# Decay factors at the inputs of a filter's layers, and tables of the way back made on GpSimd: a change to a long-convolution kernel with a second block behind it

## Chip, cores, metric

One core of one Trainium2 chip. The metric is the device time of one execution in microseconds (us), the lower the better. A time is given as the median of several executions, with the lowest and highest. Time spent in a stage is read from the profiled execution, one per run. The profiles write PE for TensorE (the matmuls), PEld for its weight loads, DVE for VectorE, ACT for ScalarE, POOL for GpSimd and SP for the queue of transfers; the granted clock is the share of TensorE's full clock that the trace records. A run counts as fast when it lies within 1.5% of the fastest of its kernel.

## The reference

```python
# x, v: (4, 12480, 128)   pos_emb: (12480, 64)   w1: (64, 64)   w2: (64, 128)
h_mlp  = np.maximum(pos_emb @ w1, 0.0) @ w2
window = np.exp(-0.01 * np.arange(S))[:, None]          # decay along the sequence
h_filt = h_mlp * window
u      = x * v
y      = irfft(rfft(u, n=2*S, axis=1) * rfft(h_filt, n=2*S, axis=0))[:, :S]
a      = (x * y).reshape(49920, 128)
h      = a @ w_in                                       # 128 -> 2048
out    = (h * np.cos(h)) @ w_out                        # 2048 -> 128
```

The decay is positive, so max(p, 0) * d = max(p * d, 0): a factor that belongs to a row may be applied to that row of `pos_emb` before the two layers. That is what the change rests on.

## The kernel before

The convolution is a Fourier transform in two steps of sizes 120 and 96, done with matmuls; its way back has two steps too. Sines and cosines ("tables") are made on the chip: each takes an angle, four small elementwise instructions that bring it into range, and a Sin on ScalarE. Everything that the change touches lies in the first 313 of 3840 us. It is made of five stages, called A to E from here on:

- **A**, the filter's layers: eleven chunks of `pos_emb` are transposed, go through `w1` and ReLU; all tables are made beside it; x * v of the first batch begins.
- **B**, the layers' output (`w2`), beside x * v.
- **C**, the first step of the filter's transform, beside the rest of x * v.
- **D**, the first step of the transform of u = x * v, beside the conversion of the second block's weights.
- **E**, the second steps of both transforms, and their product.

```python
def sines(self, row, column, turn, outs, eighths=None):          # class Tables
    base = ...                                    # VectorE: row * column
    for dst, quarters in outs:
        turned = self.pool.tile([P, P], F32, name="turned", bufs=2)
        # four VectorE instructions: moved = base + quarters; turned = moved/turn + ROUND;
        #                            turned = (turned - ROUND)*turn; turned = moved - turned
        yield
        nc.scalar.activation(dst, t, AF.Sin, scale=TWO_PI / turn)

def filter_windows(pool):                         # eleven tables of decay factors
    ...
    for i in range(NCH):
        nc.scalar.activation(w[:, :, :], first[:, :, :], AF.Exp, bias=start[:, i:i+1], scale=DECAY)

def filter_hidden(pool, bank, aT, i, peT, w1_sb, window):
    nc.tensor.matmul(pa[:, 0:ROWS * H], w1_sb[:, :], peT[:, :], start=True, stop=True)
    nc.scalar.activation(t[:, :, :], ..., AF.Relu)
    nc.gpsimd.tensor_tensor(aT[...], t[:, :, :], window[:, :, :], op=ALU.mult)

# A
for i in range(NCH):                              # NCH = 11
    if i + 1 < NCH:
        peTs[i + 1] = filter_turn(pool, bank, pes.pop(i + 1), ident)   # transposes + ScalarE copy
    filter_hidden(pool, bank, aT, i, peTs.pop(i), w1_sb, windows[i])
    for _ in range(2):
        next(sines, None)                         # two tables a round, sixteen in all
    if i >= 5:
        for _ in range(3):
            next(first_u)                         # x * v
...
# C
for i, _ in enumerate(f1_units(bank, ftile[0:FR, :, :, :], f1_evict_filter)):
    if i % 2 == 0:
        next(first_u, None)
```

An eviction copies the result of matmuls out of its accumulation bank, so that the bank can be used again. `f1_units` yields after each half of a channel pair's eviction; even pairs are evicted by ScalarE, odd ones by VectorE. `first_u` yields after each half product and after the sums of a tile of x * v.

Of the kernel before, what the change touches and what calls it, by code (L numbers as in the profile page):

```python
# [16 lines left out]
P = 128  # L17
# [13 lines left out]
def kernel(  # L31
# [62 lines left out]
    KF = N1 - (N2 - N1)  # L94
# [3 lines left out]
    assert NCH * ROWS <= FR <= R and H <= ODD and KE <= 2 * KF and H <= CB and N2 <= P  # L98
# [83 lines left out]
    class Tables:  # L182
        def __init__(self, pool):
            self.pool = pool
            self.prod, self.moved = (
                pool.tile([P, P], F32, name=name) for name in ("prod", "moved"))
# [8 lines left out]
        def sines(self, row, column, turn, outs, eighths=None):  # L195


            p, n = outs[0][0].shape
            base = self.prod[0:p, 0:n]
            nc.vector.tensor_scalar(out=base, in0=row[0:p, 0:n],  # L200
                                    scalar1=column[0:p, 0:1], scalar2=None, op0=ALU.mult)
            if eighths is not None:
                nc.vector.tensor_scalar(out=base[:, eighths], in0=base[:, eighths],
                                        scalar1=float(turn // 8), scalar2=None, op0=ALU.add)
            for dst, quarters in outs:
                turned = self.pool.tile([P, P], F32, name="turned", bufs=2)
                m, t = self.moved[0:p, 0:n], turned[0:p, 0:n]
                if isinstance(quarters, int):
                    quarters = float(quarters * turn // 4)
                nc.vector.tensor_scalar(out=m, in0=base, scalar1=quarters,  # L210
                                        scalar2=None, op0=ALU.add)

                nc.vector.tensor_scalar(out=t, in0=m, scalar1=1.0 / turn, scalar2=ROUND,
                                        op0=ALU.mult, op1=ALU.add)
                nc.vector.tensor_scalar(out=t, in0=t, scalar1=ROUND, scalar2=float(turn),
                                        op0=ALU.subtract, op1=ALU.mult)
                nc.vector.tensor_tensor(t, m, t, op=ALU.subtract)
                yield
                nc.scalar.activation(dst, t, AF.Sin, scale=TWO_PI / turn)

    def tables(pool):

        t = Tables(pool)
        part = t.whole([P, 1], [[1, 1]], channel_multiplier=1, name="part")
        part4 = t.whole([P, 1], [[1, 1]], base=1, channel_multiplier=4, name="part4")
        step = t.whole([P, P], [[1, P]], name="step")
        step4 = t.whole([P, P], [[4, P]], base=1, name="step4")
        mid = t.whole([P, P], [[1, P]], base=-MID, name="mid")
# [17 lines left out]
        yield from t.sines(step4, odd_p, 2 * TURN, [(tw_w[:, 0, :], 1), (tw_w[:, 1, :], 0)])  # L246
        cs, rows, tw_t = back_tables(pool)
# [56 lines left out]
    def filter_windows(pool):  # L304

        first = pool.tile([P, H, ROWS], F32, name="first")
        nc.gpsimd.iota(first[:, :, :], pattern=[[2, H], [N2, ROWS]], base=0,
                       channel_multiplier=0, allow_small_or_imprecise_dtypes=True)
        start = pool.tile([P, NCH], F32, name="start")
        for m in range(2):  # L310
            nc.gpsimd.iota(start[m * FO:(m + 1) * FO, :], pattern=[[ROWS * N2, NCH]], base=m,
                           channel_multiplier=0, allow_small_or_imprecise_dtypes=True)
        nc.vector.tensor_scalar(out=start[:, :], in0=start[:, :], scalar1=DECAY,
                                scalar2=None, op0=ALU.mult)
        windows = []
        for i in range(NCH):
            w = pool.tile([P, H, ROWS], F32, name=f"window{i}")
            nc.scalar.activation(w[:, :, :], first[:, :, :], AF.Exp,
                                 bias=start[:, i:i + 1], scale=DECAY)
            windows.append(w)  # L320
        return windows
# [9 lines left out]
    def filter_hidden(pool, bank, aT, i, peT, w1_sb, window):  # L331

        pa = bank()
        nc.tensor.matmul(pa[:, 0:ROWS * H], w1_sb[:, :], peT[:, :], start=True, stop=True)
        t = pool.tile([P, H, ROWS], F32, name="relu", bufs=2)
        nc.scalar.activation(t[:, :, :], pa[:, 0:ROWS * H].rearrange("p (n a) -> p a n", a=H),
                             AF.Relu)
        nc.gpsimd.tensor_tensor(aT[:, 0:H, i * ROWS:(i + 1) * ROWS], t[:, :, :],
                                window[:, :, :], op=ALU.mult)
# [67 lines left out]
    def f1_evict(ps, b, places=None):  # L407
        copy, negated = f1_takers(b)
        pj = ps[:, 0:4 * N1].rearrange("p (i r k) -> p r k i", i=2, r=2)
        for dst, k in places or ((parts, slice(0, N1)),):  # L410
            copy(out=dst[0:ODD, :, :, b, :], in_=pj[0:ODD, :, k])
        yield
        for dst, k in places or ((parts, slice(0, N1)),):
            copy(out=dst[ODD:KE, 0, :, b, :], in_=pj[ODD:KE, 1, k])
            negated(dst[ODD:KE, 1, :, b, :], pj[ODD:KE, 0, k])
        yield

    def f1_evict_filter(ps, b):
        return f1_evict(ps, b, ((fnear, slice(0, KF)), (ffar, slice(KF, N1))))

    def f2_mm(ps, w, k1, i, filt=False):

        k = k1 + i
        src = parts[:, :, k] if not filt else fnear[:, :, k] if k < KF else ffar[:, :, k - KF]
        nc.tensor.matmul(ps[0:N2, i * 2 * D:(i + 1) * 2 * D], w[:, i, :], src[0:KE],  # L425
                         start=True, stop=True)
# [304 lines left out]
    with tc.manual_schedule():  # L731
        with tc.tile_pool(name="psum", bufs=8, space=PSUM) as psum, \
# [8 lines left out]
            ffar = above.rearrange("p b (r k) i -> p r k b i", r=2)  # L741
# [6 lines left out]
            with tc.tile_pool(name="layers", bufs=1, side="right") as pool:  # L748
# [8 lines left out]
                for i in range(1, NCH):  # L757
                    pes[i] = filter_load(pool, i)
                first_u = u_units(0, 3, slots[0:R, :, :, :],
                                  lambda j, half: nc.gpsimd if half == 0 or 6 <= j < 18  # L760
                                  else nc.vector)
# [3 lines left out]
                windows = filter_windows(pool)  # L765
                sines = tables(pool)
                nc.gpsimd.memset(aT[:, 0:H, NCH * ROWS:FR], 0.0)
                peTs = {0: filter_turn(pool, bank, pes.pop(0), ident)}
                for i in range(NCH):
                    if i + 1 < NCH:  # L770
                        peTs[i + 1] = filter_turn(pool, bank, pes.pop(i + 1), ident)
                    filter_hidden(pool, bank, aT, i, peTs.pop(i), w1_sb, windows[i])
                    for _ in range(2):
                        next(sines, None)
                    if i >= 5:
                        for _ in range(3):
# [5 lines left out]
            ftile = fpool.tile([P, CB, 2 * KF, 2], F32, name="ftile")  # L782
            fnear = ftile[:, :, :, :].rearrange("p b (r k) i -> p r k b i", r=2)
            clear_gap(ftile[0:FR, :, :, :])
            with tc.tile_pool(name="out", bufs=1, side="right") as pool:
                for j in range(H // 2):
                    filter_out(pool, bank, aT, ftile, j, w2_sb)
                    for _ in range(1 + (j % 4 == 0)):
                        next(first_u)
            for i, _ in enumerate(f1_units(bank, ftile[0:FR, :, :, :], f1_evict_filter)):  # L790
                if i % 2 == 0:
                    next(first_u, None)
            for _ in first_u:
                pass
# [113 lines left out]
```

## Time and profile before

Time before: 3840.26 us (3834.36 to 3843.71, three runs); the profiled run spans 3838.6 us. The stage borders are the first matmul of each stage in the trace (of the output, the filter's first step, u's first step, the second steps, the way back). The views that carry the bounds are shown in the prediction.

| stage | begins, us | length, us | what sets its end |
|---|---|---|---|
| A layers | 0 | 52.19 | eleven exponentials, then rounds of two tables on VectorE, then GpSimd |
| B output | 52.19 | 32.03 | GpSimd |
| C filter, first step | 84.22 | 65.43 | VectorE until 122, then matmuls at half clock (0.50 from 121.70 to 147) |
| D u, first step | 149.65 | 58.02 | matmuls, VectorE and the conversion |
| E second steps | 207.67 | 105.41 | VectorE beside TensorE |
| way back of batch 0 | 313.08 | 82.95 | not touched |
| second block begins | 396.03 | | not touched |

From 15.6 to 43 us VectorE never stands for as long as 0.15 us, so it is its own work that sets the rounds. But seven times, once for each product of GpSimd's with the decay, a small instruction of VectorE's takes 1.0 to 1.9 us where its like take 0.2 to 0.3, and ends just after that product; together some 7 us (an estimate: their lengths in the trace less those of their like). One of the seven, in the timelines of GpSimd and VectorE:

```profile
24.98 1.21 POOL L338 TENSOR_TENSOR slots<-relu,window 128x480 f32<-128x480 f32 x1 [2.23 <-ACT relu L336]
25.17 1.07 DVE L210 TENSOR_SCALAR moved<-prod 120x61 f32<-120x61 f32 x1
```

### The profile page before, as it was taken

The page shows a single profiled execution, that of the slowest core. Times are in us where ns is not written, and L with a number is a line of the kernel's source. Part 1 is how long each engine was busy: PE and PEld are TensorE (multiplying, and loading weights), DVE is VectorE, ACT ScalarE, POOL GpSimd, SP SyncE. Part 2 cuts the span into 40 slices and gives each one's busy share as a digit, 9 for nine tenths or more (in the row PEclk, how much of TensorE's full clock was granted, in tenths as well). Part 3 has the DMA queues.
Part 4 walks back from the last instruction along what each step waited for, and adds up shares of the span by engine and source line. Part 5 has one row for each costly group of instructions (what it writes and reads, how often), then busy time and mean ns, then how long its engine had stood idle before and what let it go on. Part 6 is the DMA issues. An engine that isn't in the chain of part 4 may idle for free.

```text
span 3838.6 us, 47111 instructions
## 1 busy us (share of the span) xinstructions
PE 3728.1 (97%) x13450; PEld 2119.9 (55%) x13450; DVE 2819.6 (73%) x5803; ACT 2494.4 (65%) x4639; POOL 2551.1 (66%) x2274
## 2 busy tenths in 40 slices
PE   6988889999999999999999999999999999999999
PEld 4867444655556555645566556555566544444444
DVE  7888798678876787687766887788765566666666
ACT  4654566766666556766665557666654677777777
POOL 6365677478864665588845665688644577777776
PEclk8899999999999999999999999999999999999999
DMA  4253443022210561022202640122105300000000
GB/s 135 61 147 100 147 138 104 12 60 73 78 40 17 171 183 48 24 77 72 77 12 82 180 140 17 51 77 77 51 17 155 90 17 17 22 17 23 17 17 17
DMA packets 209082, 274.64 MB, mean 72 GB/s; under 512 B 17062, under 2 KB 146486, under 8 KB 208694
## 3 DMA queue, kind: packets, MB, share of 16 engines
q1 hardware_dynamic: 208822, 271.63, 24.2%
q8 instruction: 108, 1.77, 0.2%
q14 instruction: 152, 1.25, 0.1%
HBM read 191.93 MB, written 79.63 MB: 71 GB/s over the span
## 4 chain that ended last, share of the span: by engine, by line
PE 84%; DVE 5%; POOL 4%; ACT 3%; DMA 2%; issue 2%; SPq 0%; DVEq 0%; POOLq 0%; ACTq 0%
PE ph L677 32%; PE acc L702 27%; PE cv L702 5%; PE cv L468 5%; PE cv L443 4%; PE cv L395 3%; PE cv L425 3%; POOL f L686 2%; PE ph L126 2%; PE ps L395 1%; DMA hd<-h 1%; PE ps L443 1%; DVE k L683 1%; ACT cs L691 1%; DVE gt L693 1%
## 5 line engine op out<-in xcount | busy, mean ns | idle before, releaser
L686 POOL TENSOR_TENSOR f<-a,k 128x512 f32<-128x512 f32 x1568 | 1989.7, 1269 | 1065.2 <-DVE k L683 1064.1
L677 PE MATMUL ph<-at,w_in_sb 128*128 128x512 f32 x3136 | 1600.8, 592 | 20.0 <-DVE gt L693 19.6
L680 ACT ACTIVATE a<-ph,quarter 128x512 f32<-128x512 f32 x1568 | 1073.2, 684 | 746.7 <-PE ph L677 737.1
L702 PE MATMUL acc<-gt,w_out_sb 128*128 128x512 f32 x2656 | 1359.7, 593 | 5.6 <-ACT ot L708 5.3
L693 DVE TENSOR_TENSOR gt<-ph,cs 128x512 f32<-128x512 f32 x1568 | 1077.7, 687 | 326.7 <-ACT cs L691 299.3
L691 ACT ACTIVATE cs<-f 128x512 f32<-128x512 f32 x1568 | 980.3, 625 | 370.7 <-POOL f L686 369.0
L683 DVE TENSOR_SCALAR k<-a 128x512 f32<-128x512 f32 x1568 | 782.4, 499 | 595.0 <-ACT a L680 577.6
L702 PEld LDWEIGHTS acc<-gt,w_out_sb 128*128 128x128 f32 x2656 | 500.0, 189 | 650.3 <-issue 613.6
L677 PEld LDWEIGHTS ph<-at,w_in_sb 128*128 128x128 f32 x3136 | 553.2, 190 | 359.2 <-issue 262.3
L438 POOL TENSOR_TENSOR slots<-slots,t 120x256 f32<-120x256 f32 x384 | 310.7, 815 | 62.1 <-DVE t L437 23.8
L468 PEld LDWEIGHTS cv<-slots,tm 96*104 96x104 f32 x1920 | 241.5, 171 | 99.0 <-issue 86.0
L468 PE MATMUL cv<-slots,tm 96*104 96x128 f32 x1920 | 253.5, 275 | 3.8 <-DVE tm L277 3.8
L702 PE MATMUL cv<-gt,w_out_sb 128*128 128x512 f32 (+1 forms) x480 | 238.5, 579 | 1.0 <-DVE gt L693 1.0
L443 PEld LDWEIGHTS cv<-cs,slots 120*96 120x96 f32 x1536 | 176.9, 167 | 69.1 <-issue 68.7
L443 PE MATMUL cv<-cs,slots 120*96 120x120 f32 x1536 | 183.2, 266 | 0.0
L425 PE MATMUL cv<-slots,w 124*120 124x256 f32 x576 | 173.0, 380 | 0.0
L425 PEld LDWEIGHTS cv<-slots,w 124*120 124x120 f32 x576 | 103.4, 184 | 122.4 <-issue 109.7
L395 PEld LDWEIGHTS cv<-c,slots 104*124 104x124 f32 x768 | 132.7, 192 | 64.4 <-issue 58.3
L702 PEld LDWEIGHTS cv<-gt,w_out_sb 128*128 128x128 f32 x480 | 90.9, 190 | 110.2 <-issue 106.9
L395 PE MATMUL cv<-c,slots 104*124 104x192 f32 x768 | 150.9, 326 | 0.1
L383 DVE TENSOR_TENSOR xt<-xt,vt 104x256 f32<-104x256 f32 x198 | 146.7, 743 | 1.2 <-DMA vt<-in_v_dram 0.9
L453 DVE TENSOR_TENSOR slots<-cv,other 96x240 f32<-96x240 f32 x384 | 133.6, 394 | 2.8 <-ACT other L451 2.8
(116 smaller groups left out, 2549.0 us busy)
## 6 DMA issues: line engine op xcount, KB each, us to landing
h<-hd SPq DMA_DIRECT2D x144, 240.0 KB
tm<-td SPq DMA_DIRECT2D x90, 312.0 KB
xt<-in_x_dram SPq DMA_DIRECT2D x120, 208.0 KB
vt<-in_v_dram SPq DMA_DIRECT2D x120, 208.0 KB
xs<-in_x_dram SPq DMA_DIRECT2D x120, 208.0 KB
zd<-zs SPq DMA_DIRECT2D x120, 208.0 KB
zb<-zd SPq DMA_DIRECT2D x97, 256.0 KB
w<-wd SPq DMA_DIRECT2D x144, 116.2 KB
```

The costliest lines, as they stand in the source:

```text
L395: nc.tensor.matmul(ps[0:KE, i * 2 * N1:(i + 1) * 2 * N1], u[:, b, 0:KE, i], c1[0:u.shape[0], :, :].rearrange("p r k -> p (r k)"), start=Tr ...
L425: nc.tensor.matmul(ps[0:N2, i * 2 * D:(i + 1) * 2 * D], w[:, i, :], src[0:KE], start=True, stop=True)
L438: nc.gpsimd.tensor_tensor(y[:, r], y[:, r], t[:, r], op=op)
L443: nc.tensor.matmul(ps[0:N1, (i * 2 + r) * N2:(i * 2 + r + 1) * N2], parts[0:N2, r, :, b, i], cs[:, r, :], start=True, stop=True)
L468: nc.tensor.matmul(ps[0:R, i * D:(i + 1) * D], t[:, i, r, :], slots[0:N1, :, place, :], start=(r == 0), stop=(r == 1))
L677: nc.tensor.matmul(ph[:, 0:m], w_in_sb[:, c * P:(c + 1) * P], ats[n][:, 0:m], start=True, stop=True)
L680: nc.scalar.activation(a[:, 0:m], ph[:, 0:m], AF.Identity, bias=quarter[:, 0:1], scale=INV_TWO_PI)
L683: nc.vector.tensor_scalar(out=k[:, 0:m], in0=a[:, 0:m], scalar1=ROUND, scalar2=ROUND, op0=ALU.add, op1=ALU.subtract)
L686: nc.gpsimd.tensor_tensor(f[:, 0:m], a[:, 0:m], k[:, 0:m], op=ALU.subtract)
L691: nc.scalar.activation(cs[:, 0:m], f[:, 0:m], AF.Sin, scale=TWO_PI)
L693: nc.vector.tensor_tensor(gt[:, 0:m], ph[:, 0:m], cs[:, 0:m], op=ALU.mult)
L702: nc.tensor.matmul(accs[n][:, 0:m], w_out_sb[:, c, :], gt[:, 0:m], start=(c == 0), stop=(c == NFC - 1))
```

## The change

The intent has four parts. The decay goes to the inputs: one exponential instead of eleven, and VectorE multiplies each chunk of `pos_emb` in place before the transposes, so ReLU writes its result directly. Ten of the sixteen tables, those of the way back, leave A and are made on GpSimd in C, after x * v. x * v itself begins a round earlier, with a new split of its products between VectorE and GpSimd, and takes two steps a round. A new layout of the filter's tile saves one VectorE or ScalarE instruction of six per channel pair, and splits the second step's matmul in two for the values of k from 48 on.

```diff
 class Tables:
-    def __init__(self, pool):
+    def __init__(self, pool, engine):                 # every nc.vector below -> self.engine
-def tables(pool):                                     # sixteen tables
-    t = Tables(pool)
+def forward_tables(pool):                             # six
+    t = Tables(pool, nc.vector)
+def inverse_tables(pool):                             # ten
+    t = Tables(pool, nc.gpsimd)
...
-def filter_windows(pool):                             # eleven Exp
+def filter_window(pool):                              # one Exp, 120 x 88
+def filter_scale(pe, window, i):
+    w = window[:, i * ROWS:(i + 1) * ROWS]
+    spread = bass.AP(tensor=w.tensor, offset=w.offset, ap=[*w.ap, [0, FO]])
+    nc.vector.tensor_tensor(rows, rows, spread, op=ALU.mult)
...
 def filter_hidden(...):
-    nc.scalar.activation(t[:, :, :], ..., AF.Relu)
-    nc.gpsimd.tensor_tensor(aT[...], t[:, :, :], window[:, :, :], op=ALU.mult)
+    nc.scalar.activation(aT[...], ..., AF.Relu)
...
 def f1_evict_filter(ps, b):
-    return f1_evict(ps, b, ((fnear, slice(0, KF)), (ffar, slice(KF, N1))))   # six instructions
+    copy(out=near[0:ODD], in_=pj[0:ODD, 0:N1 + KF])
+    copy(out=far[0:ODD], in_=pj[0:ODD, N1 + KF:])
+    yield
+    copy(out=near[ODD:KE, 0:N1], in_=pj[ODD:KE, N1:])
+    negated(near[ODD:KE, N1:], pj[ODD:KE, 0:KF])
+    negated(far[ODD:KE], pj[ODD:KE, KF:N1])
...
 # A
-first_u = u_units(..., lambda j, half: nc.gpsimd if half == 0 or 6 <= j < 18 else nc.vector)
+first_u = u_units(..., lambda j, half: nc.vector if half and j % 3 else nc.gpsimd)
...
+for i in range(NCH + 1):
+    if i < NCH:
+        pe = pes.pop(i)
+        filter_scale(pe, window, i)
+        peTs[i] = filter_turn(pool, bank, pe, ident)
+    if i > 0:
+        filter_hidden(bank, aT, i - 1, peTs.pop(i - 1), w1_sb)
+    next(sines, None)                                 # one table a round
+    if i >= 4:
+        for _ in range(2):
+            next(first_u)
...
 # C
+f1 = f1_units(bank, ftile[0:FR, :, :, :], f1_evict_filter)
+for _ in first_u:
+    for _ in range(2):
+        next(f1)
+with tc.tile_pool(name="tables", bufs=1) as pool:
+    sines = inverse_tables(pool)
+    for i, _ in enumerate(f1):
+        if i % 5 == 0:
+            next(sines, None)
+    for _ in sines:
+        pass
```

## The prediction

> **What bounds the kernel now.** I read the page first, then the span cut at the borders between stages, then in each stage the chain of waits and each engine's timeline.
>
> ```profile
> PE 3728.1 (97%) x13450; PEld 2119.9 (55%) x13450; DVE 2819.6 (73%) x5803; ACT 2494.4 (65%) x4639; POOL 2551.1 (66%) x2274
> ```
>
> TensorE is busy 97% of the span. The diff touches nothing after the first way back begins (about 313 us), so only the opening can change. Its stages, found from where each line's matmuls begin and end (columns: stretch, length, then busy us of PE, PEld, DVE, ACT, POOL; granted clock, DMA share, GB/s):
>
> ```profile
> 0.00:52.20 52.20, 26.49 (x67) 12.98 (x67) 32.88 (x87) 23.32 (x51) 23.63 (x38) 0.74 0.43 110
> 52.20:84.20 32.00, 27.79 (x120) 20.46 (x121) 26.74 (x75) 11.05 (x30) 30.38 (x39) 0.93 0.58 168
> 84.20:121.70 37.50, 35.45 (x176) 32.95 (x176) 32.94 (x121) 25.97 (x132) 20.66 (x28) 0.86 0.46 131
> 121.70:149.65 27.95, 26.59 (x81) 23.12 (x81) 20.78 (x90) 11.49 (x60) 0.58 (x1) 0.53 0.08 28
> 149.65:207.00 57.35, 46.59 (x258) 44.68 (x256) 47.80 (x128) 40.83 (x122) 28.56 (x32) 0.93 0.15 42
> 207.00:313.00 106.00, 96.86 (x384) 67.58 (x384) 92.82 (x288) 52.91 (x138) 67.53 (x96) 0.97 0.58 169
> ```
>
> These are: A, the filter's layers (0 to 52); B, the layers' output beside x * v (52 to 84); C, the filter's first step, with x * v until 122 and alone after that; D, the same step of u; E, both second steps. B is GpSimd's (30.4 of 32.0). In C, VectorE is first the bound, then the matmuls at about half clock. The chain through A:
>
> ```profile
> 3.44 6.55 ACT window L318 x11
> 9.99 0.45 ACT peT L328
> 10.48 1.98 PE ps L334 x2
> 12.49 0.58 ACT relu L336
> 13.14 1.20 POOL slots L338
> 14.34 0.18 POOL part L190 x2
> ...
> 18.61 1.04 DVE turned L213
> ```
>
> Eleven exponentials hold ScalarE for 6.5 us, so the first copy waits until 10. GpSimd, in order, waits for the first ReLU before it makes the counts for the tables, so VectorE's tables start at 15. Eight rounds of two tables then take 3.3 us each, until 43. From 43 to 52 a third limit follows:
>
> ```profile
> 43.89 0.97 POOL L389 TENSOR_TENSOR slots<-xt 104x256 f32<-104x256 f32 x1 [2.80 <-DVE xt L383]
> 44.82 1.20 POOL L338 TENSOR_TENSOR slots<-relu,window 128x480 f32<-128x480 f32 x1
> ...
> 44.19 2.10 DVE L383 TENSOR_TENSOR xt<-xt,vt 104x256 f32<-104x256 f32 x1
> ```
>
> GpSimd runs three instructions back to back per round (3.07 us), and VectorE's product, 0.42 us elsewhere, takes 2.10 beside them.
>
> [...] VectorE's difference at 68.39 kept its 0.42 beside a GpSimd sum that began 0.04 us later and took 0.97 for 0.73[...]. [...] the matmuls of 127.83 to 149.65 run without a gap, and the clock stays at 0.50 until 147.
>
> ```profile
> 127.83 21.99 PE L395 MATMUL ps<-c,ftile 96*124 96x192 f32 x68 [1.29 <-ACT slots L402]
> ```
>
> **A, the layers.** Removed: eleven exponentials (6.55 us of ScalarE), eleven GpSimd products (11 x 1.20 = 13.2 us), and ten of sixteen tables from VectorE (24.7 to 43.1 us, x * v in between). Added: one exponential of 120x88 and eleven VectorE products of 120x512 at 0.69 us = 7.6 us. The first product can start when its input has landed (3.76 us, from the first transpose), the second at 7.05 (the second transpose's wait for DMA). From there, per round, VectorE has 0.7 + 1.2 for one table (a product or none, then four instructions at 0.24) = 1.9 us; TensorE at half clock has 0.8 for four transposes + 1.6 for the layer = 2.4, and about 1.4 at full; ScalarE 0.45 + 0.47 + 0.2 = 1.1. I take 2.2: round 6 starts at 7 + 5 x 2.2 = 18. In rounds 6 to 11 there is no table, but two thirds of an x * v tile: VectorE 0.7 + 0.5, GpSimd 1.3 to 1.4 (products 0.72 x 4/3 + sum 0.97, times 2/3). [...] 2.3 to 2.5 us. Six rounds at 2.3 end at 18 + 14 = 32, and the last ReLU at about **33**, against 52.2: **-19 us**.
>
> **B, the output.** 40 steps of x * v instead of 38, 13.3 tiles instead of 12.7. Before, a tile with both products on GpSimd takes 1.41 + 0.97 = 2.42 us. Now GpSimd has 1.9 on average, but VectorE has, per tile, 2.25 pairs of outputs at 0.69 = 1.55, plus 0.43 x 2/3 + 0.43 = 0.72, plus gaps: about 2.4. The bound changes engine but not size: 13.3 x 2.4 = 32 us. **+1 us** at most.
>
> **C, the filter's first step.** Its evictions have five instructions for six (60x192 in place of 60x144 and 60x48): from start to start 1.45 us become about 1.34 on VectorE for each odd channel pair. VectorE's products in x * v fall by a third. With x * v: 1.5 x 1.34 + 0.8 = 2.8 us a tile against 3.1; 11.7 tiles save 3.5 us. The rest are 30 channel pairs, and beside them GpSimd now makes ten tables. Its tensor_scalar costs (start to start 0.08 more):
>
> ```profile
> L135 POOL TENSOR_SCALAR power<-power 128x256 uint32<-128x256 uint32 x16 | 17.2, 1077 | 74.9 <-DVE power L133 41.3 <-DVE sig L141 33.6
> L280 POOL TENSOR_SCALAR spare<-rows,tw_t 96x208 f32<-96x208 f32 x30 | 27.0, 899 | 0.4
> L147 POOL TENSOR_TENSOR sig<-sig,low 128x256 f32<-128x256 f32 x16 | 11.6, 727 | 1.3
> ```
>
> The first two lie on one line of 0.15 us + 3.6 ns an element, though one has two operations and the other one. With the gap: 0.61 us at 104, 0.66 at 120, 0.45 at 60; a tensor_tensor 0.33 to 0.46. Four tables of 60 columns make 7.8 us, four of 104 make 9.6, two of 120 make 5.8; with four counts, 24 us. ScalarE's sine for each sits in its queue five half steps after the last, so it follows GpSimd at 2.5 pairs per 2.4 us = 0.96 us a pair, 24 us, plus some 3 for the last pairs. Before, the stretch alone took 28 (29 pairs, half clock at 1.46 us a pair once TensorE had lost its lead). So what the first part wins, the tables or the cold clock may take: **-1 us**, with room from -8 to +5.
>
> **D and E.** The raw weights now land in memory that the tables held, so their loads wait until these are stored: some 6 us after C, where the first conversion wants them 5 us into D. **+1 us.** In E the filter's matmuls for k from 48 on are split in two, 128 columns for 256: 48 more matmuls, 96 more instructions. In the way back, 100 matmuls of 120 columns pass in 10 us (320 to 330) with as many weight loads beside them, so two halves at 0.107 cost what one at 0.218 does, and E runs at VectorE's 2.04 us a step anyway (DVE 18 to 19 of every 20 us). **+1 us.**
>
> **Sum.** -19 + 1 - 1 + 1 + 1 = -17: 3840 - 17 = 3823 us.
>
> **Rivals.** (1) The gain of A is lost in C: the clock stays at half through C, or ScalarE waits for slow tables. [...] C would grow by 8 us: 3832. [...] (3) The clock stays full: then C ends with VectorE (32 x 1.34 + 9.4 + 3 = 55 us) and the tables (about 60), 5 us earlier: 3817. (4) Split matmuls bound by weight loads (0.18 each when alone): 24 steps x 0.5 less the slack of 0.3 = +5 us; the way back speaks against it.
>
> **Range and chances.** The runs of before spread by 9 us. With 8 us of doubt in A and 7 in C: 3808 to 3837 should hold it 8 times in 10. Two per cent is 77 us; faster than that would need stages A and B to vanish, slower has no cause in sight. Faster 0.01, same 0.98, slower 0.01.
>
> **What would show it.** Right: one exponential; the first output matmul at 30 to 36 us; the output stage 31 to 33 us long with VectorE busy over 90%; the tables on GpSimd 22 to 26 us long, ScalarE's sines waiting for them; E's steps at 2.04 to 2.1. Wrong: products over 1.5 us in A; the last matmul of the filter's first step more than 70 us after its first; E longer than 110 us; or a change after 313 us beyond some 5 us.

The sum keeps all its terms, -19 + 1 - 1 + 1 + 1 = -17. Two of its figures have to be read with their source. The 0.69 us of VectorE's products is the 690 ns of a 128x512 product in the profile before (L693, mean). The 2.3 us a round in A's second part is the estimate: it lays the 1.2 us of VectorE and the 1.3 to 1.4 of GpSimd mostly end to end, as at 44.19, where VectorE's product took 2.10 us beside GpSimd's work; that they always delay each other so was not shown. Rival (2) had A's products long beside GpSimd's work from the fourth round on, as at 44.19, and A ending at 42: 3833 us. Rival (1) keeps its size but not its argument, a figure for the use of TensorE that no view shows: the trace has matmuls for 8.51 of the 10 us from 106 to 116, at a clock of 1.00, then 0.59 until 121.70 and 0.50 until 147.

## The result, and the profile after

| | median, us | lowest to highest | runs |
|---|---|---|---|
| before | 3841.99 | 3834.36 to 3849.87 | 4 |
| after | 3821.43 | 3814.44 to 3823.07 | 4 |

The ratio is 0.9943, with a 95% interval of 0.9919 to 0.9967: the class is "same" by the 2% rule, though the interval excludes 1, so that a gain is clear of the noise. Here and below a ratio is that over the fast runs of both kernels, and not quite the ratio of the medians quoted. The profiled runs span 3838.6 and 3819.3 us, at a mean granted clock of 0.985 and 0.989.

The page of the kernel after, part 1, in the same columns as before (busy us, share of the span, instructions):

```profile
PE 3713.3 (97%) x13546; PEld 2117.3 (55%) x13546; DVE 2804.5 (73%) x5737; ACT 2488.4 (65%) x4597; POOL 2559.8 (67%) x2307
```

The span of the kernel after, cut at its own stage borders A to E (columns as in the prediction: stretch, length, busy us of PE, PEld, DVE, ACT, POOL; granted clock, DMA share, GB/s):

```profile
0.00:30.70 30.70, 18.13 (x67) 8.96 (x67) 17.18 (x48) 16.25 (x31) 14.26 (x25) 1.00 0.68 168
30.70:63.40 32.70, 26.11 (x120) 19.48 (x121) 30.04 (x83) 11.05 (x30) 27.57 (x32) 0.95 0.59 174
63.40:124.57 61.17, 52.83 (x256) 49.05 (x257) 51.51 (x177) 37.90 (x166) 43.45 (x81) 0.83 0.30 85
124.57:182.41 57.84, 44.50 (x257) 43.16 (x257) 48.13 (x128) 41.31 (x123) 28.59 (x32) 0.94 0.19 56
182.41:288.00 105.59, 97.22 (x480) 74.27 (x480) 91.41 (x286) 52.91 (x138) 66.78 (x94) 0.98 0.58 168
```

Stage A lost nearly 16 us of VectorE and 9 of GpSimd. In B the busiest engine is now VectorE (30.04 of 32.70 us, 92%), where it was GpSimd, at the same length. Put side by side:

| stage | before | after | predicted change | measured change |
|---|---|---|---|---|
| A | 52.19 | 30.70 | -19 | -21.5 |
| B | 32.03 | 32.70 | +1 | +0.7 |
| C | 65.43 | 61.17 | -1 | -4.3 |
| D | 58.02 | 57.84 | +1 | -0.2 |
| E | 105.41 | 106.57 | +1 | +1.2 |
| way back of batch 0 | 82.95 | 83.58 | 0 | +0.6 |
| second block, to its first finished tile | 52.51 | 55.50 | 0 | +3.0 |
| all after that | | | 0 | +1.2 |
| sum | | | -17 | -19.3 |

**A.** The chain of waits through A of the kernel after (start, length, what), against the one of before in the prediction:

```profile
7.21 0.70 DVE pe L323
...
9.01 1.63 PE ps L336 x2
...
11.25 1.28 ACT L219
...
16.65 0.83 PE ps L336 x2
```

The eleven exponentials are gone from the chain. L323 is the new product, L336 the layer, and the 1.28 us on ScalarE is the load of the Sin table, which stands before the first sine. This load makes one round long: VectorE waits 2.95 us for that sine, and the fourth product starts 4.86 us after the third. From 16 us the layer takes 0.83 us instead of 1.63, the pace of a full clock, and the first output matmul is at 30.70. (The clock column shows 1.00 for all of A; the durations say that the matmuls until about 12 us ran at half of it.) From the seventh round on x * v runs beside the products. The timelines of GpSimd and VectorE there (start, duration, engine, line, operation, count, and in brackets the idle time before and what ended it):

```profile
18.82 1.94 POOL L382 TENSOR_TENSOR xt<-xt,vt 104x256 f32<-104x256 f32 x2 [15.52 <-DMA vt<-in_v_dram]
20.84 1.57 POOL L388 TENSOR_TENSOR slots<-xt 104x256 f32<-104x256 f32 x1
22.37 1.51 POOL L382 TENSOR_TENSOR xt<-xt,vt 104x256 f32<-104x256 f32 x1
...
18.96 1.22 DVE L323 TENSOR_TENSOR pe<-pe,window 120x512 f32<-120x512 f32 x1
22.62 0.68 DVE L323 TENSOR_TENSOR pe<-pe,window 120x512 f32<-120x512 f32 x1
```

GpSimd stands until 18.82 because the first tile of v has not landed, however early the program asks for x * v. From then on it runs without a gap until 30.4, and four of its ten operations are slowed: three sums take 1.57 us where the others take 0.97, and a product 1.51 where the others take 0.70 to 0.97. VectorE's product with the decay was slowed once (1.22 for 0.69) and then kept its time; its two products of x * v took 0.95 instead of 0.42. Which of two instructions that overlap was the longer did not go with which began first: here GpSimd's product of 22.37 us took 1.51 and VectorE's, which began 0.25 us later, kept its 0.68; in the kernel before, VectorE's instruction of 25.17 us, which began 0.19 us after GpSimd's, took 1.07 for 0.2. A's end follows the landing of v: in the nine runs whose tables of the way back are off VectorE in A and whose decay is at the inputs, GpSimd's first product starts between 18.8 and 20.3 us, and A ends 10.9 to 12.1 us after it (in the kernel after 18.82 and 30.70, in e6 19.73 and 31.50). No run moved that landing.

**C.** ScalarE's and GpSimd's timelines in the kernel after, where x * v ends and the tables begin:

```profile
92.05 0.23 ACT L421 COPY slots<-ps 64x96 f32<-64x96 f32 x1
103.27 0.26 ACT L219 ACTIVATE cs<-turned 120x61 f32<-120x61 f32 x1 [10.99 <-POOL turned L217]
...
99.04 0.97 POOL L388 TENSOR_TENSOR slots<-xt 104x256 f32<-104x256 f32 x1 [0.74 <-DVE xt L382]
109.50 0.48 POOL L210 TENSOR_SCALAR moved<-prod 96x104 f32<-96x104 f32 x1
110.06 0.28 POOL L213 TENSOR_SCALAR turned<-moved 96x104 f32<-96x104 f32 x1
110.42 0.58 POOL L215 TENSOR_SCALAR turned<-turned 96x104 f32<-96x104 f32 x1
122.53 0.44 POOL L217 TENSOR_TENSOR turned<-moved,turned 96x120 f32<-96x120 f32 x1
```

GpSimd's last sum of x * v starts at 99.04; then it makes counts and tables from 100.09 to 122.97, 22.9 us. ScalarE had run ahead of it: it was done with its share of the pairs up to the first sine at 92.3, and stood there for 10.99 us. TensorE needs an empty bank for every pair. While ScalarE stands, only VectorE empties banks, and each of its evictions lets one pair through (four matmul records):

```profile
98.49 1.64 PE L394 MATMUL ps<-c,ftile 96*124 96x192 f32 x4 [1.65 <-DVE slots L403]
104.21 6.12 PE L394 MATMUL ps<-c,ftile 96*124 96x192 f32 x18 [1.72 <-ACT slots L401]
```

So TensorE's waits from 90 to 102 us are put down to VectorE (six, 4.3 us), and only that at 104.21 to ScalarE. TensorE starves, and the clock falls at about 97.5 (1.00 from 95 to 97 us, 0.50 from 98 to 104). That ScalarE's standing is behind this is shown by e3 below. A window of the same kernel over that stretch (the last three figures are clock, DMA share and GB/s):

```profile
97.00:111.00 14.00, 10.08 (x29) 9.01 (x30) 11.53 (x41) 6.67 (x29) 11.51 (x30) 0.52 0.03 9
```

**The second block's start.** Nothing there was changed, and 3 us were given back. TensorE's timeline of the kernel after, and then of the kernel before, at the same place (L691 after is L677 before, L716 is L702):

```profile
381.24 1.09 PE L126 MATMUL ph<-ident,zb 128*128 128x128 f32 x4 [2.58 <-DMA zb<-zd]
383.83 1.91 PE L691 MATMUL ph<-at,w_in_sb 128*128 128x512 f32 x2
388.31 1.02 PE L716 MATMUL acc<-gt,w_out_sb 128*128 128x512 f32 x2
```

```profile
404.88 0.63 PE L126 MATMUL ph<-ident,zb 128*128 128x128 f32 x4 [3.02 <-DVE xt L383]
407.10 1.02 PE L702 MATMUL acc<-gt,w_out_sb 128*128 128x512 f32 x2
```

Both stand for 2.6 to 3 us before the transposes. After this, the pairs of matmuls take 1.91 us in the kernel after (half clock, 0.50 from 381 to 387 us) and 1.02 in the kernel before. From the second tile to the last the distance between the two kernels stays between 18.8 and 20.2 us; it is 19.3 at the end.

### The profile page after: what moved, and what is told of

It reads as the page before. It is cut to its first block, busy times and chain, and to the rows that moved or that the text cites. A ratio compares the mean times of both kernels' runs of the same rounds, so it can differ in the third digit from the quotient of the medians.

```text
span 3819.3 us, 47226 instructions
## 1 busy us (share of the span) xinstructions
PE 3713.3 (97%) x13546; PEld 2117.3 (55%) x13546; DVE 2804.5 (73%) x5737; ACT 2488.4 (65%) x4597; POOL 2559.8 (67%) x2307
## 4 chain that ended last, share of the span: by engine, by line
PE 85%; DVE 5%; POOL 3%; DMA 3%; ACT 2%; issue 2%; SPq 0%; DVEq 0%; POOLq 0%; ACTq 0%
PE ph L691 32%; PE acc L716 28%; PE cv L716 5%; PE cv L482 5%; PE cv L457 4%; PE cv L394 3%; PE cv L433 3%; PE ph L126 2%; POOL f L700 2%; DMA hd<-h 2%; PE ps L457 1%; ACT cs L705 1%; DVE k L697 1%; PE ps L394 1%; DVE xt L382 1%
## 5 line engine op out<-in xcount | busy, mean ns | idle before, releaser
L691 PE MATMUL ph<-at,w_in_sb 128*128 128x512 f32 x3136 | 1602.7, 592 | 18.6 <-DVE gt L707 18.2
L716 PE MATMUL acc<-gt,w_out_sb 128*128 128x512 f32 x2656 | 1362.4, 594 | 5.5 <-ACT ot L722 5.3
L716 PEld LDWEIGHTS acc<-gt,w_out_sb 128*128 128x128 f32 x2656 | 500.9, 189 | 651.2 <-issue 614.1
L691 PEld LDWEIGHTS ph<-at,w_in_sb 128*128 128x128 f32 x3136 | 553.9, 190 | 358.3 <-issue 262.9
L716 PE MATMUL cv<-gt,w_out_sb 128*128 128x512 f32 (+1 forms) x480 | 238.5, 579 | 1.0 <-DVE gt L707 1.0
L716 PEld LDWEIGHTS cv<-gt,w_out_sb 128*128 128x128 f32 x480 | 90.9, 190 | 110.2 <-issue 106.9
```

The costliest lines, as they stand in the source:

```text
L691: nc.tensor.matmul(ph[:, 0:m], w_in_sb[:, c * P:(c + 1) * P], ats[n][:, 0:m], start=True, stop=True)
L716: nc.tensor.matmul(accs[n][:, 0:m], w_out_sb[:, c, :], gt[:, 0:m], start=(c == 0), stop=(c == NFC - 1))
```

## The experiments

Eleven runs, all correct against the reference: ten kernels, and the changed kernel once more. The theory to be tested: the gain is stage A's, and needs both parts; in C the tables on GpSimd are the new limit; the rest (split matmuls, share of x * v) costs little. The rivals stand in the expectations. Stages are read from one profile a run; what the same program varies by is seen in after_again. "f2" below is the moment of the first matmul of E, so the sum of A to D.

| kernel | A | B | C | D | C+D | f2 at | span |
|---|---|---|---|---|---|---|---|
| before | 52.19 | 32.03 | 65.43 | 58.02 | 123.45 | 207.67 | 3838.6 |
| after | 30.70 | 32.70 | 61.17 | 57.84 | 119.01 | 182.41 | 3819.3 |
| e1_decay_only | 51.77 | 33.23 | 50.04 | 63.07 | 113.11 | 198.11 | 3835.6 |
| e2_tables_only | 40.57 | 31.92 | 66.33 | 58.63 | 124.96 | 197.45 | 3831.7 |
| e3_sines_last | 31.08 | 33.50 | 50.29 | 69.86 | 120.15 | 184.73 | 3815.3 |
| e4_old_share | 30.57 | 34.21 | 64.40 | 58.01 | 122.41 | 187.19 | 3819.6 |
| e5_more_buffers | 38.55 | 33.40 | 50.30 | 62.95 | 113.25 | 185.20 | 3822.4 |
| e6_cs_in_layers | 31.50 | 33.55 | 58.34 | 58.37 | 116.71 | 181.76 | 3815.4 |
| e7_old_places | 31.40 | 32.77 | 64.59 | 58.43 | 123.02 | 187.19 | 3823.7 |
| e8_warm_start | 31.12 | 32.78 | 61.17 | 57.88 | 119.05 | 182.95 | 3815.9 |
| after_again | 30.96 | 32.96 | 61.07 | 58.27 | 119.34 | 183.26 | 3816.2 |
| e9_both | 31.02 | 33.34 | 52.77 | 61.39 | 114.16 | 178.52 | 3815.7 |
| e10_all | 32.14 | 33.33 | 52.76 | 61.85 | 114.61 | 180.08 | 3812.1 |

| kernel | median, us (lowest to highest, runs) | before in the same rounds | ratio (95%) |
|---|---|---|---|
| e1_decay_only | 3834.90 (3833.76 to 3837.80, 4) | 3840.44 | 0.9988 (0.9973 to 1.0003) |
| e2_tables_only | 3833.62 (3833.03 to 3838.16, 4) | 3840.44 | 0.9987 (0.9971 to 1.0004) |
| e3_sines_last | 3819.64 (3817.09 to 3822.84, 4) | 3840.44 | 0.9948 (0.9933 to 0.9963) |
| e4_old_share | 3823.62 (3821.36 to 3824.67, 4) | 3840.44 | 0.9957 (0.9942 to 0.9972) |
| e5_more_buffers | 3824.66 (one run, state unknown) | 3842.10 | |
| e6_cs_in_layers | 3816.98 (3815.47 to 3817.30, 4) | 3842.10 | 0.9929 (0.9913 to 0.9946) |
| e7_old_places | 3825.47 (one run, state unknown) | 3842.10 | |
| e8_warm_start | 3819.78 (3817.75 to 3820.60, 4) | 3842.10 | 0.9937 (0.9922 to 0.9952) |
| after_again | 3820.49 (3818.09 to 3823.01, 6) | 3841.76 | 0.9941 (0.9927 to 0.9954) |
| e9_both | 3815.58 (3811.81 to 3817.49, 4) | 3841.76 | 0.9926 (0.9911 to 0.9940) |
| e10_all | 3813.91 (3812.36 to 3814.49, 5) | 3841.76 | 0.9922 (0.9907 to 0.9937) |

### e1_decay_only: the change, with the ten tables back on VectorE in A

```diff
-    t = Tables(pool, nc.gpsimd)
+    t = Tables(pool, nc.vector)                        # in inverse_tables
-sines = forward_tables(pool)
+sines = itertools.chain(forward_tables(pool), inverse_tables(pool))
-    next(sines, None)
+    for _ in range(2):
+        next(sines, None)
 # and in C, no tables: "for _ in f1: pass"
```

> The changed kernel, but the ten tables of the way back are made on VectorE in the layers' stage again, as before the change (two tables a round). Theory: the decay at the inputs and the move of the tables win separately. The layers' stage then has 8 rounds of 0.65 + 2.5 us instead of 2 us, so its end moves from 30.7 to about 41 to 43 us; the filter's first step loses its tables and with them ScalarE's wait, so it shrinks from 61.2 to about 56. At the start of the second steps the kernel is then some 6 us behind the changed one (182.4 becomes 187 to 190), in all 12 to 16 us faster than before. Rival (the tables' move is nearly the whole gain): the layers' stage ends at 48 or later and the kernel is within 6 us of before.

A took 51.77 us: the theory missed, and the rival it named for A held. The decay at the inputs, here with the new share of x * v and the new layout, gains 0.4 us in A. Timelines of ScalarE and VectorE of this kernel, over one of the rounds:

```profile
33.97 0.56 ACT L331 COPY peT<-ps 128x480 f32<-128x480 f32 x1 [2.44 <-PE ps L127]
...
32.06 0.68 DVE L324 TENSOR_TENSOR pe<-pe,window 120x512 f32<-120x512 f32 x1
36.30 0.21 DVE L214 TENSOR_SCALAR turned<-moved 96x104 f32<-96x104 f32 x1 [2.33 <-ACT rows L220]
```

Read as a ring: VectorE's product at 32.06 releases the transposes, these release ScalarE's copy at 33.97, the layer and the ReLU follow, and only behind them in ScalarE's queue come the round's two sines, at 35.99. VectorE at 36.30 has waited 2.33 us for a sine, because the table it is about to write goes into one of two `turned` buffers, which the sine has to free. Only after that comes the next product. A round takes 4.89 us (27.17 to 32.06 from product to product), longer than the 3.3 us of before, where no product of VectorE's stood ahead of the transposes. So the new product lengthens the very loop that the old tables keep, which the theory's expectation didn't see. (VectorE's small instructions, seven of which took 1.0 to 1.9 us beside GpSimd's products before, take 0.2 to 0.3 us in this round.) In C + D, on the other hand, this kernel has 113.11 us, 10.3 less than before: what C and D take when no tables lie beside them.

### e5_more_buffers: e1 with six `turned` buffers instead of two

```diff
-turned = self.pool.tile([P, P], F32, name="turned", bufs=2)
+turned = self.pool.tile([P, P], F32, name="turned", bufs=6)
```

> The kernel of the run that kept the tables on VectorE in the layers' stage (first output matmul at 51.8 us), with six buffers for the sines' inputs instead of two. There each round took 4.9 us: the second table of a round waits 1.5 to 2.3 us for the sine that frees its buffer, and that sine queues on ScalarE behind a copy and a ReLU that hang on VectorE's own product of the same round. Theory: the ring of VectorE, TensorE, ScalarE through two buffers costs the 10 us, not the tables' work; with six buffers a round is 0.65 + 2.5 = 3.2 us and the output begins at 38 to 43 us. [...]

(The rival had A stay at 49 to 52 us, with VectorE's own work as one limit.) A fell from 51.77 to 38.55 us, within what the buffers' theory expected: the ring is through the buffers. (More buffers in the kernel before were not tried; there VectorE hardly waits in these rounds, so they have no wait to remove.) It also says what moving the tables to GpSimd buys beyond that. Against e5, the kernel after is 7.9 us shorter in A and 0.7 in B, and 5.8 longer in C + D (119.01 against 113.25): it is at f2 only 2.8 us earlier.

### e2_tables_only: before, with only the ten tables moved to GpSimd in C

```diff
-sines = tables(pool)
+sines = forward_tables(pool)                           # Tables as in the change
-    for _ in range(2):
-        next(sines, None)
+    next(sines, None)
 # and C as in the change; the windows and GpSimd's products stay
```

> The kernel before, with only the tables of the way back moved to GpSimd beside the filter's first step (one table a round in the layers' stage). Theory: the exponentials still hold the first copy until 10 us and GpSimd still makes eleven products, so from round 5 on GpSimd sets 3.07 us a round; the layers' stage ends at 43 to 46 us instead of 52.2. The filter's first step has the same wait of ScalarE for GpSimd's tables as the changed kernel and lasts 60 to 65 us. In all 5 to 11 us faster than before. Rival (the tables on VectorE were what held the layers' stage): it ends at 38 or earlier and most of the changed kernel's gain is there.

A took 40.57 us, 11.6 less than before: below the 43 to 46 expected and above the rival's 38. C took 66.33 us, above the 60 to 65 expected, and C + D grew by 1.5 us over before: the old eviction is still there and the tables are added. With e1 this makes the square in A complete, if one leaves aside that e1 has the new share and layout too (taken out of the changed kernel alone, by e4 and e7, they move A by -0.1 and +0.7): decay alone -0.4, tables alone -11.6, both -21.5. The parts alone add up to -12.0, which is 9.5 us short of both together. The whole kernels follow: 0.9988 and 0.9987 for the parts (both intervals contain 1), 0.9943 for the change.

### e3_sines_last: the change, with the ten sines only after the filter's last pair

```diff
-turned = self.pool.tile([P, P], F32, name="turned", bufs=2)
+turned = self.pool.tile([P, P], F32, name="turned", bufs=10 if late else 2)
...
-    yield
-    nc.scalar.activation(dst, t, AF.Sin, scale=TWO_PI / turn)
+    if late: self.owed.append((dst, t, TWO_PI / turn))
+    yield
+    if not late: nc.scalar.activation(dst, t, AF.Sin, scale=TWO_PI / turn)
 # all owed sines after the last unit of f1
```

> The changed kernel, but ScalarE's ten sines of the way back are emitted after the last unit of the filter's first step, with ten buffers between, so no eviction queues behind a sine that waits for GpSimd. Theory: the 11 us in which ScalarE stands before the first sine (92 to 103 us) starve TensorE of banks and bring the half clock at 97 to 111; without them the first step of the filter is bound by VectorE and lasts 55 to 58 us instead of 61.2; the sines then wait for GpSimd's last table once (ScalarE free again at about 123 to 125 us), which u's first step pays with 0 to 2 us. In all 2 to 6 us faster than the changed kernel. Rival: VectorE's backlog or the half clock sets the end of the stage anyway; then it stays at 60 to 62 us and the total within 1 us.

C became 10.9 us shorter, even more than the theory of ScalarE's wait expected, but D 12.0 longer, so the expected 2 to 6 us for the whole were missed: C + D is 120.15 us against 119.01. Lines of ScalarE's timeline and of the table of waits of this kernel (114 to 185 us; who waited, for whom, in total, times, longest):

```profile
124.07 0.30 ACT L267 ACTIVATE tw_t<-turned 96x120 f32<-96x120 f32 x1 [1.89 <-POOL turned L218]
...
PE ps L401 <- ACT slots L408: 8.5, 1, 8.5
```

Now ScalarE waits for GpSimd's last table at the end instead of for the first one at the beginning, TensorE waits 8.5 us for it, and ScalarE begins D's evictions only at 124.39. In C TensorE now waits 1.7 us in all for ScalarE and 0.8 for VectorE (its start aside), and the clock stays at 1.00 from 84 to 116 us: so it was ScalarE's standing that starved TensorE in the kernel after. Yet the time only moved on into D; the wait at the front is therefore not itself the cost. What sets the end is GpSimd's chain, x * v to 100 and then 23 us of tables, wherever the sines stand.

### e6_cs_in_layers: the four smaller tables on GpSimd already in A

```diff
+def cs_tables(pool):                                   # the four tables of 60 columns,
+    t = Tables(pool, nc.gpsimd, lag=2)                 # each sine two rounds after its table
+    ...
 # A, once a round:
     next(sines, None)
+    next(more, None)                                   # more = cs_tables(pool)
 # in C, six tables are left
```

> The changed kernel, with four of the ten tables of the way back (the 60-column ones, 8.6 us of GpSimd) made on GpSimd in the layers' stage, where it has nothing to do from 3.3 to 18.8 us; their sines follow two rounds later. Six remain beside the filter's first step. Theory: from the last x * v tile (about 100 us) GpSimd's tables are the chain that ends the filter's first step and holds ScalarE, whatever the place of the sines; with 15 us of them for 24, that step and u's first step together take 112 to 116 us instead of 119[...]. In all 3 to 7 us faster than the changed kernel. Rival (VectorE's evictions and the conversions of u's first step set the sum): the two steps stay at 118 to 120.

C + D fell to 116.71 us, against 119.01, and just missed the range expected; A cost 0.8 us (31.50 against 30.70; 0 to 2 were expected). The whole kernel takes 3816.98 us. The shorter chain pays, as the reading of e3 says it must, but ScalarE still stands before its first sine of C; the waits of this kernel from 64 to 122 us:

```profile
ACT rows L226 <- POOL turned L218: 12.1, 3, 10.9
```

### e9_both: e6, with the six remaining sines last, and the addition written as x * 1.0 + c

```diff
-self.engine.tensor_scalar(out=m, in0=base, scalar1=quarters, scalar2=None, op0=ALU.add)
+self.engine.tensor_scalar(out=m, in0=base, scalar1=1.0, scalar2=quarters,
+                          op0=ALU.mult, op1=ALU.add)   # where quarters is a number
 # e6's six tables in C: sines after the last unit of f1, as in e3
```

> The changed kernel with both: four tables in the layers' stage on GpSimd, and the six remaining sines only after the last unit of the filter's first step; besides, the addition of a quarter turn is written as times 1 plus a constant, since GpSimd's times-and-plus took 0.28 us on 96x104 where its plus alone took 0.48. Theory: each alone left the other's wait (alone, the later sines moved the wait into u's first step; alone, the fewer tables left ScalarE standing 10.9 us before the first sine). Together GpSimd is done at 115 to 117 us, when VectorE ends the filter's first step; that step and u's take 108 to 112 us instead of 119, and the kernel is 6 to 11 us faster than the changed one. Rival (u's first step is bound by the conversions started late): the two take 115 or more.

C + D is 114.16 us, against 119.34 in the run of the changed kernel beside it (after_again): 5.2 us won, though not the 108 to 112 expected. That range was set below what there was to win, for e1 and e5, without any tables in C, have 113.1 and 113.3; e9 has all but 1 us of it. What each of the three parts of the edit gives in e9 isn't separated. The odd part of it shows in GpSimd's timeline of this kernel, a line to be compared with the one at 109.50 of the kernel after, which took 0.48 us for the same addition on the same shape:

```profile
102.19 0.27 POOL L212 TENSOR_SCALAR moved<-prod 96x104 f32<-96x104 f32 x1
```

The end is less clear than the stage: of the 6 us that e9 was ahead where the second block begins, only 0.5 us are left in the two profiled spans, since that block took 54.68 us to its first tile instead of 52.58 and lost more by 555 us. The timed runs show 3815.58 against 3820.49 us, and their ranges don't overlap.

### e4_old_share: the change, with x * v shared as before

```diff
-lambda j, half: nc.vector if half and j % 3 else nc.gpsimd
+lambda j, half: nc.gpsimd if half == 0 or 6 <= j < 18 else nc.vector
```

> The changed kernel with the old share of x * v between GpSimd and VectorE (second halves on GpSimd for tiles 6 to 17, on VectorE for the others). Theory: the output stage is 32 to 33.5 us either way, bound by GpSimd at 2.42 us a tile instead of by VectorE, and the filter's first step is 1 to 2 us longer because VectorE has every second half there; in all 0 to 3 us slower than the changed kernel. Rival (the spread share is what made room): the output stage grows by over 3 us.

B became 1.5 us and C 3.2 us longer, 4.8 at f2, more than the 0 to 3 expected. With the old split every second half of the tiles from 18 on lies on VectorE, which in C has the evictions too. In the profiled span it doesn't show: that is 3819.6 us, as in the kernel after, because in this run the second block started in 52.30 us and not in 55.50. In the timed runs the median is 16.8 us below before of the same rounds, where the changed kernel's is 20.6 and 21.3 below; the intervals of the ratios overlap.

### e7_old_places: the change, with the old layout of the filter's tile and unsplit matmuls

```diff
-KF = N1 - 2 * (N2 - N1)
+KF = N1 - (N2 - N1)
 # f1_evict, f1_evict_filter and f2_mm as before: six instructions a pair, one matmul for all k
```

> The changed kernel with the filter's old places: six evictions a channel pair, one matmul of 256 columns for every k. Theory: 1.45 us for 1.36 on VectorE per odd pair, so the stretch with x * v grows by some 1.6 us and with it the start of the tables; the filter's first step 62 to 64 us instead of 61.2, the second steps unchanged at 105 to 107.5 us whatever the matmuls, since VectorE sets them. Rival (split matmuls cost): the second steps fall below 105.

C took 64.59 us instead of 61.17, a little above the range expected, so the sixth instruction was worth 3.4 us there. E took 106.34, against 106.57 with the split matmuls: a cost of the split doesn't show, and the 5 us of the prediction's fourth rival are ruled out.

### e8_warm_start: the change, with unread matmuls before the second block's first transposes

```diff
 load(0)
+keep_warm(10)                # 128x512 matmuls of w_in with itself; nobody reads the result
 moe_turn(mpool, 0)
...
+if c == LAG - 1 and n == 0:
+    keep_warm(3)
```

> The changed kernel with thirteen matmuls more whose result nobody reads, ten while TensorE waits for the first rows of the second block and three while it waits for the next ones. Theory: the 3 us that the changed kernel gave back between the second block's first matmul and its first finished tile (55.5 us for 52.5) are half clock at 382 to 387; with TensorE kept busy that stretch is 49 to 52.5 us, and the kernel 2 to 6 us faster. Rival (a transfer or a wait holds the stretch): it stays at 55 to 56 us while the clock is full.

TensorE's timeline of this kernel:

```profile
376.29 3.48 PE L872 MATMUL ph<-w_in_sb 128*128 128x512 f32 x6
...
383.11 1.02 PE L716 MATMUL acc<-gt,w_out_sb 128*128 128x512 f32 x2
```

After the unread matmuls the real ones take 1.02 us, and the clock in the stretch to the first finished tile is 1.00 where the kernel after has 0.93. The stretch took 53.16 us, more than the 49 to 52.5 expected, though the block also began 2.5 us earlier (81.08 us after the way back's start, not 83.58). From f2 to the first finished tile this makes 4.4 us less than in the kernel after. After_again has the same program as the kernel after, no unread matmuls, and 52.58 us for the same stretch at a clock of 0.99. The stretch in the kernel after, in after_again and in e8 (columns as before):

```profile
372.56:428.06 55.50, 48.81 (x179) 27.06 (x178) 46.96 (x80) 32.34 (x65) 39.20 (x37) 0.93 0.47 137
373.42:426.00 52.58, 45.54 (x179) 25.00 (x178) 46.63 (x80) 32.32 (x65) 39.66 (x37) 0.99 0.49 145
371.07:424.23 53.16, 47.90 (x186) 25.79 (x184) 47.14 (x82) 33.17 (x68) 38.23 (x37) 1.00 0.48 143
```

So the 3 us that the change seemed to give back differ between two runs of the same program, and are not the change's. The lower clock goes with them here, but that it alone sets the stretch isn't shown: e3 has 52.34 us at 0.96. Nor is it shown that unread matmuls make the kernel faster: the medians, 3819.78 us and 3820.49 in after_again, are from different rounds, and the ratios are 0.9937 and 0.9941.

### after_again: the changed kernel once more, beside e9 and e10

> The changed kernel once more, for rounds shared with the two that follow. Theory: the stages' borders repeat to a few tenths of a us except where the clock differs; 0.994 to 0.995 of the kernel before.

A to D repeat within 0.5 us each, and so does E; the second block's start is 2.9 us shorter. Beside the kernel before of the same rounds the median is 21.3 us lower (ratio 0.9941).

### e10_all: e9, with the unread matmuls and a third `turned` buffer for the tables of A

```diff
-t = Tables(pool, nc.vector)
+t = Tables(pool, nc.vector, lag=1)      # in forward_tables: one sine later, three buffers
 # and keep_warm as in e8
```

> The previous one with the matmuls [...] at the start of the second block, and with a third buffer and one round of delay for the forward tables' sines, so that VectorE doesn't stand 2.9 us in the third round. Theory: the second block's start wins 3 to 4 us as before, the layers' stage 0 to 2.5 us; 9 to 16 us faster than the changed kernel, 0.990 to 0.992 of the kernel before. Rival: the layers' stage is then held by x * v's first transfer (18.8 us) and wins nothing.

A didn't gain: 32.14 us against 31.02 in e9. Its rounds end with x * v on GpSimd, which here starts when v has landed at 20.26 us, and A ends 11.9 us later, as in the kernel after; so an earlier table has nothing to move, as the rival had it. The test isn't a clean one, though: the third buffer didn't remove VectorE's wait for the first sine, it came one table later and took 3.43 us. The rest adds up: 3813.91 us, the best of all, 6.6 us under the changed kernel by the medians of the same rounds (3820.49), with ranges that don't overlap, and 27.9 under the kernel before.

## Why the prediction was right

The predicted 3823 us stand against 3821.43, the predicted -17 against -19.3 in the profiled spans and -20.6 in the medians. That the spans agree so well is in part luck: up to the way back the change won 24.1 us and not 17, because A and C each won more than they were to, and in the profiled run 4.8 us that no step had were given back behind it. In after_again the same two figures are 23.7 and 1.3. By its steps:

- **A, predicted -19, measured -21.5. Mechanism right in the main, one term too large and one bound missed.** The first part of the sum held as a whole: round 6 was to start at 18, and its product started at 18.96, after four rounds of 1.5 to 2.0 us and one of 4.86 for the 2.2 expected. The second part, six rounds at 2.3 us and a last ReLU, was to end at 33; it ended at 30.70. The six rounds are 1.9 us each, (30.56 - 18.96)/6. The estimate had laid VectorE's and GpSimd's work mostly end to end, 2.3 to 2.5; four of GpSimd's ten operations were longer by 0.6 to 0.8 us, but its share took no more than 11.6 us, and VectorE's products, after one of 1.22 us, kept their 0.68. Two waits that no step had: that for the first sine, with its table load, 2.95 us at 9.9, which was regained because the rounds behind it were short; and that for the first tile of v, until 18.82. That the sum's 18 for the seventh product and the landing of v lie so close together is chance.
- **B, +1, measured +0.7. Right,** and for the reason given: the bound moved to VectorE at 92% of the stage.
- **C, -1 with room from -8 to +5, measured -4.3.** The tables' length was right, 24 us predicted, 22.9 measured. The line it came from (0.15 us + 3.6 ns an element, whatever the operation) was wrong for each operation and right in the sum, 0.48, 0.28 and 0.58 us for 0.53 each. The sign "ScalarE's sines waiting for them" came true, too. What failed is "ScalarE follows GpSimd at 0.96 us a pair": it left out that ScalarE was far ahead when x * v ended on GpSimd, and first stood for 11 us. e3 shows that this wait is not a cost by itself. The two terms of the sum were mis-sized in opposite ways. Cut where GpSimd's last sum of x * v ends (122.28 us before, 100.01 after), the stretch with x * v became 1.5 us shorter, where the prediction had 3.5, and the rest 2.8 us shorter, where it had 2.5 us of loss. Taken out of the changed kernel alone, the new layout is worth 2.6 us in that first stretch (e7) and the new share 1.1 (e4), together about what the prediction had; over the whole of C they are worth 3.4 and 3.2. Why the first stretch, with both in, is only 1.5 us shorter than before stays open.
- **D, +1, measured -0.2, and E, +1, measured +1.2.** Neither size says anything about its reason. The later loads cost D nothing that shows: they are issued at 125.05 us, the first conversion starts 5.4 us into D, before the change 5.7, and no engine's wait in D is put down to them. In E the reason given is not borne out: e7 has unsplit matmuls and 106.34 us. Over all kernels E varies from 105.41 to 107.67 us, in no relation to the form of its matmuls (unsplit: 105.41, 106.34, 107.05); why, stays open.
- **Nothing after 313 us, "beyond some 5 us", measured +4.8.** Within the limit. 3 us of it lie at the second block's start, shown by after_again to vary from run to run.

The rivals: (1), the half clock in C, came true in part (0.52 from 97 to 111 us, and ScalarE's wait for the tables), but not at the cost of 8 us. (2), A's products slow beside GpSimd's until 42 us, is refuted by 30.70. (3), the full clock throughout, had the length of C about right (60 us; measured 61.17). Its premise is refuted by that same 0.52, but its bound, the tables, ended where it said, 59.6 us after C's first matmul. (4), split matmuls bound by their weight loads, is refuted by e7.

Where did the gain that was to be had go? Without tables in C, C + D would take 113 us; with ten of them on GpSimd it takes 119. So about 6 of the 21.5 us won in A are paid back in C, as GpSimd's serial chain after x * v. This loss lies inside the predicted net of -1 and didn't show in it. e6 recovers 2.3 us of it and e9 5.2.

## What to carry to other kernels

Work that is moved ahead within a loop can close a ring through a small pool of buffers: the change alone then shows nothing, and only with the other change, or with more buffers, does the gain show (-0.4 us alone, -13.6 with six buffers, -21.5 with the tables gone). Before moving work to "the engine that is idle there", ask when that engine becomes free in program order and whether the moved chain, started then, ends the stage; time that is won at one place and lost again at the next (e3: 10.9 and 12.0 us) tells that the place of the wait was not the cause. And when one run shows a loss in code that was not touched, run the same kernel again before explaining it.
